# Sharing each gate/up chunk between the two row groups of TensorE, one chunk apart, in a spectral-mixing block with a GeGLU feed-forward

## The chip, the cores and the metric

One core of a Trainium2 chip; the sessions of experiments ran on three different chips. The metric is the device time of one execution in microseconds (us); lower is better. Executions of one kernel vary here by some 0.5%, so medians of several runs are given, and ratios are taken within one session on one chip; where times of different sessions are put side by side, the text says so. A trace is one execution under the profiler; its "span" runs from the first to the last instruction and lies 1.8 to 3.5 us (mostly 2.2) below the device time of the same execution. The engines are PE (TensorE, matmuls), DVE (VectorE), ACT (ScalarE), POOL (GpSimd) and SP (SyncE); SBUF is the memory on the core, PSUM the memory into which PE writes its sums, in banks. "Warm" means on the full granted clock of PE, "cold" on half of it.

## The reference, cut to what matters

```python
S, D, F = 2048, 576, 4608
x  = A_x                                              # bf16 [1, 2048, 576]
X  = rfft2(layernorm(x)) * (w_r + 1j * w_i)           # spectral mixing
h  = x + irfft2(X, s=(S, D))
n  = layernorm(h)
h2 = h + (gelu(n @ w_gate) * (n @ w_up)) @ w_down     # GeGLU feed-forward
```

The feed-forward (FFN) takes more than four fifths of the time. The size D = 576 over which gate and up sum is 4.5 times 128, or nine tiles of 64 features.

## The kernel before: the parts that matter

The spectral stage is built from matmuls with tables. Each of 16 groups passes D (columns), B (a 16-point transform and the weight multiply on DVE) and V (a 16-point inverse); V lags D by two groups:

```python
ZS = sb.alloc("ZS", [128, 2, 2, ZW], BF16)            # double buffer between B and V
for i in range(NG + 2):
    if i < NG:        st_D(i)
    if 1 <= i <= NG:  st_B(i - 1)                     # writes ZS[i % 2] on DVE
    if i >= 2:        st_V(i - 2)                     # PE reads ZS
```

Then 16 row tiles of 128 tokens pass the inverse stages `st_I` and `st_N` and the second layernorm. For the first block of 512 tokens, PE turns the normalised tile (`turn_pe`), DVE copies it out of PSUM, and two copies SBUF to SBUF double the activations, so that each of the nine 64-feature tiles lies on partitions 0-63 and again on partitions 64-127:

```python
HT0 = sb.alloc("HT0", [128, 9, 512], BF16)
def turn_pe(c):
    ...                                               # five 128x128 turns on PE into PSUM
    DVE: HT0[:, 0:5, t0:t1] <- PSUM                   # written short
    P.dma(SP, HT0[0:64, 5:9, t0:t1],   HT0[64:128, 0:4, t0:t1], ...)   # the doubling copies
    P.dma(SP, HT0[64:128, 5:9, t0:t1], HT0[0:64, 1:5, t0:t1], ...)
```

Blocks 2 to 4 are turned by nine DMA transposes a tile, while the block before them computes. The weights of gate lie on partitions 0-63, those of up on 64-127. Both are loaded early, from two queues, in nine pieces of 512 columns; the down weights follow on the POOL queue as soon as the spectral stage has freed their space:

```python
for j in range(9):
    f0, f1 = 512 * j, 512 * j + 512
    P.dma(POOL, WGU[0:64, :, f0:f1],   wgv[:, :, f0:f1], ...)
    P.dma(SP,   WGU[64:128, :, f0:f1], wuv[:, :, f0:f1], ...)
for j in range(9):
    P.dma(POOL, WD[:, 4 * j:4 * j + 4, :], wdv[...], ...)
```

A chunk is 128 of the 4608 inner features for 512 tokens. Gate runs on rows 0-63 of the array and up on rows 64-127, as nine pairs of matmuls that run at the same time into two PSUM banks:

```python
def gu(n, tb, f):
    b0 = 2 * (n % 3)
    for kt in range(9):
        for o in range(2):                            # 0: gate, 1: up
            h0, sl = 64 * o, (GT, UT)[o][kt]
            matmul(bank(b0 + o), WGU[h0:h0+64, kt, 128*f:128*f+128], HT[h0:h0+64, sl, :],
                   start=(kt == 0), stop=(kt == 8))
    if n == 0: st_N(15)                               # the last 128-point inverse
    ACT: GL <- gelu(bank(b0));   DVE: AT[:, f, :] <- GL * bank(b0 + 1)
```

36 chunks make a block; then `down` multiplies AT with the down weights (288 matmuls of 288 columns) and the output is stored. There are four blocks.

Of the kernel before, what the change touches and what calls it, by code (L numbers as in the profile page):

```python
# [4 lines left out]
BF16 = mybir.dt.bfloat16  # L5
# [137 lines left out]
class Prog:  # L143
# [12 lines left out]
    def op(self, eng, fn, r=(), w=(), dma=None):  # L156
# [6 lines left out]
        for k in w:  # L163
            for o in self.last_w.get(k, ()):
                deps.add((o, "waw"))
            for o in self.readers.get(k, ()):
                deps.add((o, "war"))
        op = _Op(eng, fn, deps, dma)
# [27 lines left out]
    def emit(self):  # L196
# [8 lines left out]
        for op in self.all:  # L205
            kn = known[op.eng]
            cand = {}
            for o, kind in op.deps:
                if o.dma is not None:
                    key, v = ("d", o.dma), o.val  # L210
                else:
                    if o.eng == op.eng and op.dma is None:
                        if op.eng == "pe":
                            continue
                    key, v = ("e", o.eng), o.pos + 1
                if v > kn.get(key, 0):
                    if key not in cand or v > cand[key][0]:
                        cand[key] = (v, o)
# [64 lines left out]
def _build(nc, A_x, A_w_r, A_w_i, B_w_gate, B_w_up, B_w_down, out):  # L283
# [39 lines left out]
    HT0 = sb.alloc("HT0", [128, 9, 512], BF16)  # L323
# [15 lines left out]
    ZS = sb.alloc("ZS", [128, 2, 2, ZW], BF16)  # L339
# [3 lines left out]
    HT1 = sb.alloc("HT1", [128, 9, 512], BF16)  # L343
# [189 lines left out]
    def st_B(i):  # L533
# [14 lines left out]
        P.op(DVE, lambda v, sl=sl: v.tensor_tensor(ZS[:, sl, 0, 0:KW], T1[:, sl, 0, :], T1[:, sl, 1, :], op=ALU.subtract), r=[("T1", sl)], w=[("Z", sl, 0)])  # L548
        P.op(DVE, lambda v, sl=sl: v.tensor_tensor(ZS[:, sl, 1, 0:KW], T2[:, sl, 0, :], T2[:, sl, 1, :], op=ALU.add), r=[("T2", sl, 0), ("T2", sl, 1)], w=[("Z", sl, 1)])  # L549

    def st_V(i):
        g = GORD[i]
        sl = i % 2
# [18 lines left out]
    for i in range(NG + 2):  # L572
# [4 lines left out]
        if i >= 2:  # L577
            st_V(i - 2)


    wgv = B_w_gate[:, :].rearrange("(t p) f -> p t f", p=64)
    wuv = B_w_up[:, :].rearrange("(t p) f -> p t f", p=64)
    wdv = B_w_down[:, :].rearrange("(c p) d -> p c d", p=128)
    for j in range(9):
        f0, f1 = 512 * j, 512 * j + 512
        P.dma(POOL, WGU[0:64, :, f0:f1], wgv[:, :, f0:f1], f"wg{j}", w=[("WG", j, 0)])
        P.dma(SP, WGU[64:128, :, f0:f1], wuv[:, :, f0:f1], f"wu{j}", w=[("WG", j, 1)])
# [3 lines left out]
    P.alias(["FT", "BT", "VT"], [("HT", 0, i, k) for i in range(4) for k in range(3)])  # L591
# [43 lines left out]
    def norm(c):  # L635
        hs = c % 2
        q = c // 4
        for i, (o0, o1, x0, x1) in enumerate(((0, D, 0, D), (D, 640, 0, 64))):
# [4 lines left out]
    def turn_dma(c):  # L643
# [3 lines left out]
        for k in range(9):  # L647
            o = 128 * k if k < 5 else 64 + 128 * (k - 5)
            P.dma(SP, HT[:, k, 128 * (c % 4):128 * (c % 4) + 128], HN[:, hs, o:o + 128], f"tr{c}",
                  r=[("HN", hs, 0), ("HN", hs, 1)], w=[("HT", q % 2, c % 4, k)], transpose=True)  # L650

    def turn_pe(c):
# [8 lines left out]
        P.dma(SP, HT0[0:64, 5:9, t0:t1], HT0[64:128, 0:4, t0:t1], f"tr{c}", r=[("HT", 0, c, 0)], w=[("HT", 0, c, 1)])  # L661
        P.dma(SP, HT0[64:128, 5:9, t0:t1], HT0[0:64, 1:5, t0:t1], f"tr{c}", r=[("HT", 0, c, 0)], w=[("HT", 0, c, 2)])

# [17 lines left out]
    fdead += [("T1", a) for a in range(2)] + [(n_, a, b_) for n_ in ("T2", "Z") for a in range(2) for b_ in range(2)]  # L681
    fnew = ([("AT", f) for f in range(36)] + [("GL", 0), ("GL", 1)] + [("HT", 1, i, k) for i in range(4) for k in range(9)])

    GT = (0, 5, 1, 6, 2, 7, 3, 8, 4)
    UT = (4, 0, 5, 1, 6, 2, 7, 3, 8)

    def gu(n, tb, f):
        b0 = 2 * (n % 3)
        HT = HTS[tb % 2]
        rk = [("HT", tb % 2, i, k) for i in range(4) for k in range(9)] + [("WG", f // 4, i) for i in range(2)]  # L690
        for kt in range(9):
            for o in range(2):
                h0, sl = 64 * o, (GT, UT)[o][kt]
                P.op(PE, lambda t, o=o, h0=h0, kt=kt, sl=sl, f=f, b0=b0, HT=HT: t.matmul(  # L694
                    bank(b0 + o), WGU[h0:h0 + 64, kt, 128 * f:128 * f + 128], HT[h0:h0 + 64, sl, :], start=(kt == 0), stop=(kt == 8)),
                    r=rk, w=[("PS", b0 + o)])
        if n == 0:
            st_N(NT - 1)
            P.alias(fdead, fnew)
        s2 = n % 2  # L700
# [4 lines left out]
    def down(tb, p):  # L705
        b0 = 6 - 2 * (p % 2)
        c = 4 * tb + p
        for h in range(2):
            for f in range(36):
                P.op(PE, lambda t, b0=b0, h=h, f=f, p=p: t.matmul(bank(b0 + h, 0, 128, 0, 288), AT[:, f, 128 * p:128 * p + 128],  # L710
                                                                  WD[:, f, 288 * h:288 * h + 288], start=(f == 0), stop=(f == 35)),
                     r=[("AT", f), ("WD", f // 4)], w=[("PS", b0 + h)])
            P.op(DVE, lambda v, b0=b0, h=h, p=p, c=c: v.tensor_tensor(OS[:, p % 2, 288 * h:288 * h + 288], bank(b0 + h, 0, 128, 0, 288),  # L713
                                                                      XO[:, c, 288 * h:288 * h + 288], op=ALU.add),
                 r=[("PS", b0 + h), ("X", c)], w=[("OS", p % 2, h)])
            P.dma(SP, ov[:, c, 288 * h:288 * h + 288], OS[:, p % 2, 288 * h:288 * h + 288], f"so{p % 2}{h}", r=[("OS", p % 2, h)], w=[("OUT", p % 2, h)])

    for tb in range(4):
        for f in range(36):
            gu(36 * tb + f, tb, f)  # L720
# [46 lines left out]
```

## Time and profile before

Median 527.12 us of three runs (525.86 to 527.65). The traced execution took 529.1 us, with a span of 526.9 us.

| stretch of the trace | from-to, us | what bounds it |
|---|---|---|
| spectral stage (D, B, V) | 21.6-65.2 | PE, but for 1.0 us at its start and about 2 us of waits at its end |
| inverse stages and layernorm | 65.2-90.7 | PE |
| nothing on PE | 90.7-98.8 | the doubling copies |
| FFN block 1, gate/up | 98.8-172.5 | PE, at first on half the clock |
| down 1, then blocks 2 to 4 | 172.5-526.9 | PE |

From the page of the kernel before: the span, each engine's busy time, the granted TensorE clock and the GB/s moved in 40 slices of 13.2 us, the chain that ended last, and the two groups of gate/up matmuls (busy us, mean ns of one, idle time just before them and what ended it). HT_69 is HT0 in the code, HT_84 is HT1; in later traces both are called HT.

```profile
span 526.9 us, 10210 instructions
...
PE 507.8 (96%) x4425; PEld 302.5 (57%) x4427; DVE 184.1 (35%) x428; ACT 152.8 (29%) x285; POOL 29.1 (6%) x49
...
PEclk9999999699999999999999999999999999999999
...
GB/s 289 247 208 230 220 268 316 68 11 26 26 25 7 13 18 18 11 26 24 26 9 12 17 18 11 27 27 26 6 12 18 18 1 1 0 1 2 12 18 18
...
PE PS L694 51%; PE PS L710 27%; PE PS L525 4%; PE PS L601 3%; SPq L191 2%; DMA XO<-in_A_x_dram 2%; PE PS L539 1%; SPq L193 1%; PE PS L558 1%; ACT U L453 1%; DMA HT_69<-HT_69 1%; PE PS L610 1%; PE PS L562 1%; DVE XO L613 1%; DMA HT_84<-HN 0%
...
L694 PE MATMUL PS<-HT_69,WGU 64*128 64x512 bf16 x1296 | 143.3, 380 | 8.2 <-DMA HT_69<-HT_69 8.1
...
L694 PE MATMUL PS<-HT_84,WGU 64*128 64x512 bf16 x1296 | 140.2, 376 | 0.0
```

PE is busy 96% of the span, and gate/up (L694) and down (L710) carry 78% of the chain. The one idle time of note stands in the first gate/up group: 8.1 us, ended by a DMA from HT to itself, that is, by a doubling copy. In the same slice, the eighth, the clock digit falls to 6. PE's waits from 60 to 110 us (total, times, longest) say it again, and show the end of the spectral stage:

```profile
PE PS L694 <- DMA HT_69<-HT_69: 8.1, 1, 8.1
PE PS L558 <- ACT YS L542: 0.8, 1, 0.8
PE PS L558 <- DVE ZS L549: 0.6, 1, 0.6
PE PS L601 <- ACT V L565: 0.5, 1, 0.5
```

The timeline of PE (start, length, operation, count) shows the hole between the last inverse matmul of the loop and the first gate/up, and behind it 18 matmuls in 4.02 us where a warm chunk takes 1.94:

```profile
90.29 0.41 PE L610 MATMUL PS<-GS,IT 128*128 128x288 bf16 x2
98.81 4.02 PE L694 MATMUL PS<-HT_69,WGU 64*128 64x512 bf16 x18 [8.11 <-DMA HT_69<-HT_69]
```

Stretches of the FFN (length, then busy time and count of PE, weight loads, DVE, ACT and POOL; then granted clock, DMA share and GB/s): the first 6.2 us run at a clock of 0.54, the rest at 1.00.

```profile
98.80:105.00 6.20, 6.20 (x30) 2.08 (x32) 0.77 (x2) 0.74 (x2) 0.00 (x0) 0.54 0.01 3
105.00:172.00 67.00, 66.92 (x621) 29.74 (x618) 26.58 (x47) 24.88 (x40) 0.00 (x0) 1.00 0.09 19
208.00:278.00 70.00, 70.00 (x649) 31.18 (x646) 26.63 (x44) 20.90 (x35) 0.00 (x0) 1.00 0.09 19
```

And the DMA issues of the weights and copies (count, size of one, median us from issue to landing):

```profile
WGU<-in_B_w_up_dram SPq DMA_DIRECT2D x9, 576.0 KB, 31.7
WD<-in_B_w_down_dram POOLq DMA_DIRECT2D x9, 576.0 KB, 18.0
...
HT_69<-HT_69 SPq DMA_DIRECT2D x8, 64.0 KB, 7.4
```

A copy of 64 KB takes 7.4 us in the median, from 3.5 to 17.1. By the trace's record of landings the last up load lands at 96.83 and the last copy at 98.45 us.

### The profile page before, as it was taken

How to read it: one execution, taken by the hardware profiler on the slowest of the kernel's cores; microseconds unless marked ns; L12 is line 12 of the kernel's file. 1: busy time of each engine (PE TensorE's matmuls, PEld its weight loads, DVE VectorE, ACT ScalarE, POOL GpSimd, SP SyncE). 2: the span in 40 equal slices, each digit the busy share in tenths (PEclk: the TensorE clock that was granted, in tenths of full speed). 3: DMA queues.
4: the chain of work that ended last, by engine and by line, in shares of the span. 5: the costliest groups of instructions: out<-in, count | busy, mean ns of one | idle time of the engine just before them, and what ended most of it. 6: DMA issues, size and time to landing. Idle time of an engine off the chain costs nothing.

```text
span 526.9 us, 10210 instructions
## 1 busy us (share of the span) xinstructions
PE 507.8 (96%) x4425; PEld 302.5 (57%) x4427; DVE 184.1 (35%) x428; ACT 152.8 (29%) x285; POOL 29.1 (6%) x49
## 2 busy tenths in 40 slices
PE   7899898499999999999999999999999999999997
PEld 3667576144444777444447774456677744444776
DVE  5677658044433111343331114433311133333111
ACT  5756578042343000223330002333300023333000
POOL 8800130000000000000000000000000000000000
PEclk9999999699999999999999999999999999999999
DMA  8999999401110000011100000111000000000000
GB/s 289 247 208 230 220 268 316 68 11 26 26 25 7 13 18 18 11 26 24 26 9 12 17 18 11 27 27 26 6 12 18 18 1 1 0 1 2 12 18 18
DMA packets 36812, 30.76 MB, mean 58 GB/s; under 512 B 21296, under 2 KB 32752, under 8 KB 36768
## 3 DMA queue, kind: packets, MB, share of 16 engines
q1 hardware_dynamic: 33312, 17.79, 14.8%
q0 software_dynamic: 3312, 11.80, 8.8%
q8 instruction: 35, 0.57, 0.5%
q10 hardware_dynamic: 144, 0.52, 0.3%
q14 instruction: 9, 0.07, 0.1%
HBM read 23.67 MB, written 2.36 MB: 49 GB/s over the span
## 4 chain that ended last, share of the span: by engine, by line
PE 88%; SPq 3%; DVE 3%; DMA 3%; ACT 2%; issue 1%; DVEq 0%; ACTq 0%
PE PS L694 51%; PE PS L710 27%; PE PS L525 4%; PE PS L601 3%; SPq L191 2%; DMA XO<-in_A_x_dram 2%; PE PS L539 1%; SPq L193 1%; PE PS L558 1%; ACT U L453 1%; DMA HT_69<-HT_69 1%; PE PS L610 1%; PE PS L562 1%; DVE XO L613 1%; DMA HT_84<-HN 0%
## 5 line engine op out<-in xcount | busy, mean ns | idle before, releaser
L701 ACT ACTIVATE GL<-PS 128x512 bf16<-128x512 f32 x144 | 85.8, 597 | 294.5 <-PE PS L694 293.0
L702 DVE TENSOR_TENSOR AT<-GL,PS 128x512 bf16<-128x512 bf16 x144 | 98.6, 687 | 167.1 <-ACT GL L701 167.1
L694 PE MATMUL PS<-HT_69,WGU 64*128 64x512 bf16 x1296 | 143.3, 380 | 8.2 <-DMA HT_69<-HT_69 8.1
L710 PE MATMUL PS<-WD,AT 128*128 128x288 bf16 x1152 | 141.8, 286 | 0.0
L694 PE MATMUL PS<-HT_84,WGU 64*128 64x512 bf16 x1296 | 140.2, 376 | 0.0
L710 PEld LDWEIGHTS PS<-WD,AT 128*128 128x128 bf16 x1152 | 112.4, 98 | 29.9 <-issue 1.7
L694 PEld LDWEIGHTS PS<-HT_69,WGU 64*128 64x128 bf16 x1296 | 70.8, 95 | 79.8 <-issue 11.7
L694 PEld LDWEIGHTS PS<-HT_84,WGU 64*128 64x128 bf16 x1296 | 62.6, 94 | 77.1 <-issue 0.5
L713 DVE TENSOR_TENSOR OS<-PS,XO 128x288 bf16<-128x288 f32 x32 | 14.6, 458 | 123.8 <-PE PS L710 123.8
L601 PE MATMUL PS<-DT,V 128*128 128x288 bf16 x160 | 22.0, 286 | 0.5 <-ACT V L565 0.5
L525 PE MATMUL PS<-FT,U 128*128 128x289 bf16 x160 | 22.3, 287 | 0.2 <-ACT U L453 0.2
L613 DVE SCALAR_TENSOR_TENSOR XO<-PS,XO 128x576 bf16<-128x576 f32 x16 | 12.1, 756 | 20.0 <-PE PS L610 19.8
L601 PEld LDWEIGHTS PS<-DT,V 128*128 128x128 bf16 x160 | 15.4, 98 | 4.3 <-issue 0.6
L525 PEld LDWEIGHTS PS<-FT,U 128*128 128x128 bf16 x160 | 14.4, 97 | 5.1 <-issue 0.4
L616 ACT ACTIVATE SQ<-XO 128x576 bf16<-128x576 bf16 x16 | 10.9, 682 | 15.3 <-DVE XO L613 15.1
L639 DVE TENSOR_SCALAR HN<-XO,TM,RS_59 128x576 bf16<-128x576 bf16 (+1 forms) x32 | 10.2, 360 | 8.8 <-DMA HT_84<-HN 6.4
L434 PE MATMUL PS<-ZD 128*128 128x512 bf16 x37 | 10.9, 447 | 1.5 <-POOL ZD L356 1.3
L558 PE MATMUL PS<-VT,ZS 128*128 128x256 bf16 x64 | 9.6, 271 | 2.4 <-DVE ZS L549 1.6
L405 DVE BATCH_NORM_STATS2 ST_53<-XO 128x6 f32<-128x288 bf16 x24 | 9.2, 443 | 5.5 <-DMA XO<-in_A_x_dram 5.5
L544 DVE TENSOR_TENSOR T_79<-YS,WS 128x580 bf16<-128x580 bf16 x16 | 7.4, 460 | 10.4 <-ACT YS L542 10.4
L603 ACT ACTIVATE GS<-PS 128x576 bf16<-128x576 f32 x16 | 10.2, 636 | 2.6 <-PE PS L601 2.6
L542 ACT ACTIVATE YS<-PS 128x578 bf16<-128x578 f32 x16 | 10.5, 655 | 1.5 <-PE PS L539 0.3
(57 smaller groups left out, 171.8 us busy)
## 6 DMA issues: line engine op xcount, KB each, us to landing
WGU<-in_B_w_gate_dram POOLq DMA_DIRECT2D x9, 576.0 KB, 25.8
WGU<-in_B_w_up_dram SPq DMA_DIRECT2D x9, 576.0 KB, 31.7
WD<-in_B_w_down_dram POOLq DMA_DIRECT2D x9, 576.0 KB, 18.0
out_dram<-OS SPq DMA_DIRECT2D x32, 72.0 KB, 1.6
XO<-in_A_x_dram SPq DMA_DIRECT2D x3, 576.0 KB, 8.0
HT_84<-HN SPq DMA_TRANSPOSE x72, 2.4
FT<-c_ftab SPq DMA_DIRECT2D x1, 725.0 KB, 12.5
DT<-c_dtab SPq DMA_DIRECT2D x1, 720.0 KB, 24.4
```

The source lines that it names most:

```text
L191: fn = lambda e: e.dma_start(out_ap, in_ap, transpose=True)
L434: P.op(PE, lambda t: t.matmul(bank(7), ZD[:, 0:128], ZD[:, :], start=True, stop=True), r=["ZD"], w=[("PS", 7)])
L525: P.op(PE, lambda t, b=b, o=o, dt=dt, g=g: t.matmul(bank(b, 0, 128, 0, K2), U[:, dt, g, :, :], FT[:, dt, o, 0:K2], start=(dt == 0), stop=( ...
L558: P.op(PE, lambda t, c=c, zp=zp, sl=sl, sp_=sp_: t.matmul(bank(6, 0, 128, 256 * c, 256 * c + 256), ZS[:, sl, zp, 128 * c:128 * c + 128], V ...
L601: P.op(PE, lambda t, b=b, h=h, kt=kt, c=c: t.matmul(bank(b, 0, 128, 0, 288), V[:, kt, c, :, :], DT[:, kt, 288 * h:288 * h + 288], start=(k ...
L613: P.op(DVE, lambda v, x2=x2, c=c: v.scalar_tensor_tensor(x2, banks(4, 2, 288), 1.0, x2, op0=ALU.mult, op1=ALU.add, accum_out=SB2[:, 0, c:c ...
L616: P.op(ACT, lambda a, sl=sl, c=c: a.activation(SQ[:, sl, :], XO[:, c, :], ACTF.Square, accum_out=SB2[:, 1, c:c + 1]), r=[("X", c)], w=[("S ...
L694: P.op(PE, lambda t, o=o, h0=h0, kt=kt, sl=sl, f=f, b0=b0, HT=HT: t.matmul(bank(b0 + o), WGU[h0:h0 + 64, kt, 128 * f:128 * f + 128], HT[h0 ...
L701: P.op(ACT, lambda a, s2=s2, b0=b0: a.activation(GL[:, s2, :], bank(b0), ACTF.Gelu_apprx_tanh), r=[("PS", b0)], w=[("GL", s2)])
L702: P.op(DVE, lambda v, s2=s2, b0=b0, f=f: v.tensor_tensor(AT[:, f, :], GL[:, s2, :], bank(b0 + 1), op=ALU.mult), r=[("GL", s2), ("PS", b0 + ...
L710: P.op(PE, lambda t, b0=b0, h=h, f=f, p=p: t.matmul(bank(b0 + h, 0, 128, 0, 288), AT[:, f, 128 * p:128 * p + 128], WD[:, f, 288 * h:288 * ...
L713: P.op(DVE, lambda v, b0=b0, h=h, p=p, c=c: v.tensor_tensor(OS[:, p % 2, 288 * h:288 * h + 288], bank(b0 + h, 0, 128, 0, 288), XO[:, c, 28 ...
```

## The change

Its intent: let each 64-feature tile be used where it lies, so that only the last one is needed twice. Even tiles stand on partitions 0-63, odd ones on 64-127, for gate and up alike; the ninth stands on both (the layernorm writes it twice), and rows 0-63 use it for gate, rows 64-127 for up. Rows 0-63 do the even half of a chunk's gate and up sums, rows 64-127 the odd half, into the same PSUM banks. So that both are never in one bank at once, rows 64-127 work one chunk behind, and PE waits on its own earlier matmul before the second half enters a bank. The doubling copies go, five transposes a tile take the place of nine, and the weights are loaded in four pieces over all 128 partitions. Apart from that, V lags three groups, and down's second pair of banks is 2 and 3 instead of 4 and 5. The diff is cut, and long calls are shortened.

```diff
-    HT0 = sb.alloc("HT0", [128, 9, 512], BF16)
+    HT0 = sb.alloc("HT0", [128, 5, 512], BF16)
-    ZS = sb.alloc("ZS", [128, 2, 2, ZW], BF16)
+    ZS = sb.alloc("ZS", [128, 3, 2, ZW], BF16)
...
-    for i in range(NG + 2):
+    for i in range(NG + 3):
...
-        if i >= 2:
-            st_V(i - 2)
+        if i >= 3:
+            st_V(i - 3)
...
-    for j in range(9):
-        f0, f1 = 512 * j, 512 * j + 512
-        P.dma(POOL, WGU[0:64, :, f0:f1], wgv[:, :, f0:f1], ...)
-        P.dma(SP, WGU[64:128, :, f0:f1], wuv[:, :, f0:f1], ...)
+    for j in range(4):
+        f0, f1 = 1152 * j, 1152 * j + 1152
+        for o, (eng, src) in enumerate(((POOL, B_w_gate), (SP, B_w_up))):
+            P.dma(eng, WGU[:, 4*o:4*o+4, f0:f1], src[0:512, f0:f1].rearrange("(t p) f -> p t f", p=128), ...)
+            P.dma(eng, WGU[64*o:64*o+64, 8, f0:f1], src[512:576, f0:f1], ...)
...
-        for k in range(9):                            # turn_dma
+        for k in range(5):
...
-        P.dma(SP, HT0[0:64, 5:9, t0:t1], HT0[64:128, 0:4, t0:t1], ...)
-        P.dma(SP, HT0[64:128, 5:9, t0:t1], HT0[0:64, 1:5, t0:t1], ...)
...
+    ASEQ = [(0, i) for i in range(4)] + [(0, 8)] + [(1, 4 + i) for i in range(4)]    # (gate/up, weight slot)
+    BSEQ = [(0, i) for i in range(4)] + [(1, 4 + i) for i in range(4)] + [(1, 8)]
+    def gu(n):
+        for j in range(9):
+            for half, m in ((0, n), (1, n - 1)):      # rows 64-127 are one chunk behind
+                if not 0 <= m < 144:
+                    continue
+                o, wt = (ASEQ, BSEQ)[half][j]
+                b = 2 * (m % 3) + o
+                aft = [half_done[m, o]] if half and (j == 0 or j == 4) else []       # PE waits on PE
+                op = matmul(bank(b), WGU[h0:h0+64, wt, ...], HT[h0:h0+64, kt, :],
+                            start=(half == 0 and j in (0, 5)), stop=(half == 1 and j in (3, 8)), after=aft)
+                if half == 0:
+                    half_done[m, o] = op
+        m = n - 1
...                                                   # gelu and product of chunk m
+    gu(0)                                             # one call more: half empty at both ends
     for tb in range(4):
         for f in range(36):
-            gu(36 * tb + f, tb, f)
+            gu(36 * tb + f + 1)
```

More of the change, by code (lines that the diff above doesn't have):

```diff
@@ L154, in __init__, with op @@
         self.dma_sems = {}
-    def op(self, eng, fn, r=(), w=(), dma=None):
+    def op(self, eng, fn, r=(), w=(), dma=None, after=()):
         if eng == "pool" and fn is not None and dma is None:
@@ L167, in op @@
                 deps.add((o, "war"))
+        for o in after:
+            deps.add((o, "self"))
         op = _Op(eng, fn, deps, dma)
@@ L212, in emit @@
                     if o.eng == op.eng and op.dma is None:
-                        if op.eng == "pe":
+                        if op.eng == "pe" and kind != "self":
                             continue
@@ L342, in _build @@
     AT = sb.alloc("AT", [128, 36, 512], BF16)
-    HT1 = sb.alloc("HT1", [128, 9, 512], BF16)
+    HT1 = sb.alloc("HT1", [128, 5, 512], BF16)
     GL = sb.alloc("GL", [128, 2, 512], BF16)
@@ L547, in st_B @@
                  r=[("Y", sl)] + wk, w=[("T2", sl, pl)])
-        P.op(DVE, lambda v, sl=sl: v.tensor_tensor(ZS[:, sl, 0, 0:KW], T1[:, sl, 0, :], T1[:, sl, 1, :], op=ALU.subtract), r=[("T1", sl)], w=[("Z", sl, 0)])
-        P.op(DVE, lambda v, sl=sl: v.tensor_tensor(ZS[:, sl, 1, 0:KW], T2[:, sl, 0, :], T2[:, sl, 1, :], op=ALU.add), r=[("T2", sl, 0), ("T2", sl, 1)], w=[("Z", sl, 1)])
+        P.op(DVE, lambda v, sl=sl: v.tensor_tensor(ZS[:, i % 3, 0, 0:KW], T1[:, sl, 0, :], T1[:, sl, 1, :], op=ALU.subtract), r=[("T1", sl)], w=[("Z", i % 3, 0)])
+        P.op(DVE, lambda v, sl=sl: v.tensor_tensor(ZS[:, i % 3, 1, 0:KW], T2[:, sl, 0, :], T2[:, sl, 1, :], op=ALU.add), r=[("T2", sl, 0), ("T2", sl, 1)], w=[("Z", i % 3, 1)])
     def st_V(i):
         g = GORD[i]
-        sl = i % 2
+        sl = i % 3
         sp_ = 1 if g == 0 else 0
@@ L576, in _build @@
             st_B(i - 1)
-        if i >= 2:
-            st_V(i - 2)
-    wgv = B_w_gate[:, :].rearrange("(t p) f -> p t f", p=64)
-    wuv = B_w_up[:, :].rearrange("(t p) f -> p t f", p=64)
+        if i >= 3:
+            st_V(i - 3)
     wdv = B_w_down[:, :].rearrange("(c p) d -> p c d", p=128)
-    for j in range(9):
-        f0, f1 = 512 * j, 512 * j + 512
-        P.dma(POOL, WGU[0:64, :, f0:f1], wgv[:, :, f0:f1], f"wg{j}", w=[("WG", j, 0)])
-        P.dma(SP, WGU[64:128, :, f0:f1], wuv[:, :, f0:f1], f"wu{j}", w=[("WG", j, 1)])
+    for j in range(4):
+        f0, f1 = 1152 * j, 1152 * j + 1152
+        for o, (eng, src) in enumerate(((POOL, B_w_gate), (SP, B_w_up))):
+            P.dma(eng, WGU[:, 4 * o:4 * o + 4, f0:f1], src[0:512, f0:f1].rearrange("(t p) f -> p t f", p=128), f"wgu{o}{j}", w=[("WG", j, o)])
+            P.dma(eng, WGU[64 * o:64 * o + 64, 8, f0:f1], src[512:576, f0:f1], f"wgu{o}{j}", w=[("WG", j, 2 + o)])
     P.alias(ukeys + wkeys[0] + wkeys[1] + ["Wz", ("CU", 0), ("CU", 1), ("SU", 0), ("SU", 1)], [("WD", j) for j in range(9)])
@@ L590, in _build @@
         P.dma(POOL, WD[:, 4 * j:4 * j + 4, :], wdv[:, 4 * j:4 * j + 4, :], f"wd{j}", w=[("WD", j)])
-    P.alias(["FT", "BT", "VT"], [("HT", 0, i, k) for i in range(4) for k in range(3)])
+    P.alias(["FT", "BT", "VT"], [("HT", 0, i, k) for i in range(4) for k in range(5)])
     vkeys = [("V", g) for g in range(NG)] + [("Vt", g) for g in range(NG)]
@@ L637, in norm @@
         q = c // 4
-        for i, (o0, o1, x0, x1) in enumerate(((0, D, 0, D), (D, 640, 0, 64))):
+        for i, (o0, o1, x0, x1) in enumerate(((0, D, 0, D), (D, 640, 512, D))):
             P.op(DVE, lambda v, c=c, hs=hs, o0=o0, o1=o1, x0=x0, x1=x1: v.tensor_scalar(HN[:, hs, o0:o1], XO[:, c, x0:x1], TM[:, 1, c:c + 1],
@@ L646, in turn_dma @@
         HT = HTS[q % 2]
-        for k in range(9):
-            o = 128 * k if k < 5 else 64 + 128 * (k - 5)
-            P.dma(SP, HT[:, k, 128 * (c % 4):128 * (c % 4) + 128], HN[:, hs, o:o + 128], f"tr{c}",
+        for k in range(5):
+            P.dma(SP, HT[:, k, 128 * (c % 4):128 * (c % 4) + 128], HN[:, hs, 128 * k:128 * k + 128], f"tr{c}",
                   r=[("HN", hs, 0), ("HN", hs, 1)], w=[("HT", q % 2, c % 4, k)], transpose=True)
@@ L660, in turn_pe @@
              r=[("PS", 6), ("PS", 7)], w=[("HT", 0, c, 0)])
-        P.dma(SP, HT0[0:64, 5:9, t0:t1], HT0[64:128, 0:4, t0:t1], f"tr{c}", r=[("HT", 0, c, 0)], w=[("HT", 0, c, 1)])
-        P.dma(SP, HT0[64:128, 5:9, t0:t1], HT0[0:64, 1:5, t0:t1], f"tr{c}", r=[("HT", 0, c, 0)], w=[("HT", 0, c, 2)])
     for c in range(NT + 1):
@@ L680, in _build @@
     fdead = vkeys + ["DT", "IT", ("G", 0), ("G", 1), ("Y", 0), ("Y", 1), "Yz", "Zz", ("SQ", 0), ("SQ", 1)]
-    fdead += [("T1", a) for a in range(2)] + [(n_, a, b_) for n_ in ("T2", "Z") for a in range(2) for b_ in range(2)]
-    fnew = ([("AT", f) for f in range(36)] + [("GL", 0), ("GL", 1)] + [("HT", 1, i, k) for i in range(4) for k in range(9)])
-    GT = (0, 5, 1, 6, 2, 7, 3, 8, 4)
-    UT = (4, 0, 5, 1, 6, 2, 7, 3, 8)
-    def gu(n, tb, f):
-        b0 = 2 * (n % 3)
-        HT = HTS[tb % 2]
-        rk = [("HT", tb % 2, i, k) for i in range(4) for k in range(9)] + [("WG", f // 4, i) for i in range(2)]
-        for kt in range(9):
-            for o in range(2):
-                h0, sl = 64 * o, (GT, UT)[o][kt]
-                P.op(PE, lambda t, o=o, h0=h0, kt=kt, sl=sl, f=f, b0=b0, HT=HT: t.matmul(
-                    bank(b0 + o), WGU[h0:h0 + 64, kt, 128 * f:128 * f + 128], HT[h0:h0 + 64, sl, :], start=(kt == 0), stop=(kt == 8)),
-                    r=rk, w=[("PS", b0 + o)])
-        if n == 0:
+    fdead += [("T1", a) for a in range(2)] + [(n_, a, b_) for n_ in ("T2", "Z") for a in range(3) for b_ in range(2)]
@@ new lines, in _build @@
+    fnew = ([("AT", f) for f in range(36)] + [("GL", 0), ("GL", 1)] + [("HT", 1, i, k) for i in range(4) for k in range(5)])
+    ASEQ = [(0, i) for i in range(4)] + [(0, 8)] + [(1, 4 + i) for i in range(4)]
+    BSEQ = [(0, i) for i in range(4)] + [(1, 4 + i) for i in range(4)] + [(1, 8)]
+    half_done = {}
+    def gu(n):
[3 more added lines that the diff above has]
+                    continue
+                tb, f = m // 36, m % 36
+                o, wt = (ASEQ, BSEQ)[half][j]
+                kt = 4 if wt == 8 else wt % 4
+                h0 = 64 * half
+                HT = HTS[tb % 2]
+                b = 2 * (m % 3) + o
+                aft = [half_done[m, o]] if half and (j == 0 or j == 4) else []
+                op = P.op(PE, lambda t, h0=h0, kt=kt, wt=wt, f=f, b=b, HT=HT, s=(half == 0 and j in (0, 5)), e=(half == 1 and j in (3, 8)): t.matmul(
+                    bank(b), WGU[h0:h0 + 64, wt, 128 * f:128 * f + 128], HT[h0:h0 + 64, kt, :], start=s, stop=e),
+                    r=[("HT", tb % 2, i, k) for i in range(4) for k in range(5)] + [("WG", f // 9, i) for i in range(4)],
+                    w=[("PS", b)], after=aft)
+                if half == 0:
+                    half_done[m, o] = op
+        m = n - 1
+        if m < 0:
@@ L698, in gu @@
             st_N(NT - 1)
             P.alias(fdead, fnew)
-        s2 = n % 2
+            return
+        s2, b0, f = m % 2, 2 * (m % 3), m % 36
         P.op(ACT, lambda a, s2=s2, b0=b0: a.activation(GL[:, s2, :], bank(b0), ACTF.Gelu_apprx_tanh), r=[("PS", b0)], w=[("GL", s2)])
@@ L705, in down @@
     def down(tb, p):
-        b0 = 6 - 2 * (p % 2)
         c = 4 * tb + p
         for h in range(2):
+            b = (6, 7, 2, 3)[2 * (p % 2) + h]
             for f in range(36):
-                P.op(PE, lambda t, b0=b0, h=h, f=f, p=p: t.matmul(bank(b0 + h, 0, 128, 0, 288), AT[:, f, 128 * p:128 * p + 128],
-                                                                  WD[:, f, 288 * h:288 * h + 288], start=(f == 0), stop=(f == 35)),
-                     r=[("AT", f), ("WD", f // 4)], w=[("PS", b0 + h)])
-            P.op(DVE, lambda v, b0=b0, h=h, p=p, c=c: v.tensor_tensor(OS[:, p % 2, 288 * h:288 * h + 288], bank(b0 + h, 0, 128, 0, 288),
-                                                                      XO[:, c, 288 * h:288 * h + 288], op=ALU.add),
-                 r=[("PS", b0 + h), ("X", c)], w=[("OS", p % 2, h)])
+                P.op(PE, lambda t, b=b, h=h, f=f, p=p: t.matmul(bank(b, 0, 128, 0, 288), AT[:, f, 128 * p:128 * p + 128],
+                                                                WD[:, f, 288 * h:288 * h + 288], start=(f == 0), stop=(f == 35)),
+                     r=[("AT", f), ("WD", f // 4)], w=[("PS", b)])
+            P.op(DVE, lambda v, b=b, h=h, p=p, c=c: v.tensor_tensor(OS[:, p % 2, 288 * h:288 * h + 288], bank(b, 0, 128, 0, 288),
+                                                                    XO[:, c, 288 * h:288 * h + 288], op=ALU.add),
+                 r=[("PS", b), ("X", c)], w=[("OS", p % 2, h)])
             P.dma(SP, ov[:, c, 288 * h:288 * h + 288], OS[:, p % 2, 288 * h:288 * h + 288], f"so{p % 2}{h}", r=[("OS", p % 2, h)], w=[("OUT", p % 2, h)])
+    gu(0)
     for tb in range(4):
         for f in range(36):
-            gu(36 * tb + f, tb, f)
+            gu(36 * tb + f + 1)
             if tb == 0 and f == 20:
```

## The prediction

> **What bounds the kernel now.** TensorE. The page gives PE 96% busy; the chain of waits puts 51% of 526.9 us on gate/up matmuls and 27% on down. Gate (rows 0-63) and up (rows 64-127) already run as pairs: in the timeline a pair starts every 215.5 ns when warm, so a chunk of nine pairs takes 1.945 us and a block of 36 takes 70.04 us (blocks 2 to 4 agree within 0.07 us). The Trainium skill, "TensorE: Matmul & The Clock Gate" (Back-to-back issue gap), gives 216 ns for 512 columns; the trace agrees. The change keeps nine slots per chunk, so the steady rate cannot improve. Down (122.5 ns each, 35.4 us per block) is untouched. What can be won lies outside the steady state:
>
> 1. Before the first gate/up matmul PE idles 8.1 us (waits view: on the DMA HT<-HT). DVE had the activations at 89.45 us, but the eight doubling copies queue behind the last up-weight loads, which land at 96.83; the last copy lands at 98.45.
> 2. That idle time halves the granted clock until about 104.5 us (PEclk row). The first block takes 73.67 us to its first down matmul instead of 70.04. The inserted last 128-point inverse explains 0.53; some 3.1 us are cold clock (pairs at 425 ns) and one 0.24 us stall at 139 us, where DVE's norm waited for a tile's nine transposes (1.25 us each).
> 3. In the spectral stage PE waits 1.0 us for the first ZS (26.5 to 27.46), then 0.8, 0.6 and 0.5 us at the drain (62 to 65.2). Between, a step takes 2.51 us and is PE-bound.
>
> **What the change does.**
> - No doubling copies: the first chunk needs DVE's HT and the first weight piece. That piece is larger (1152 columns), but from the first loads' landings I estimate it to land near 60 us. The loop's last matmul starts at 90.41, so the chunk can start at 90.6: -8.2 us.
> - No idle time, so no cold clock; five transposes instead of nine (6.3 us against 7.8 us between norms) remove the DVE stall: -3.1 us.
> - Lag 3 fills the first wait; the drain is 0.2 us worse through the single V bank: -0.8 us.
> - Skew: 145 calls of nine slots instead of 144: +1.94 us.
> - Two PE-on-PE waits per chunk, needed because row groups must not meet in a bank (the skill, "TensorEngine Tiling (Array Packing)", Gotcha 1). The awaited matmul lies four pairs back (0.86 us); a matmul takes 0.38 us and ACT starts about 0.1 us after PE, so I estimate 0.5 us to spare: 0.
> - Evacuation of a chunk has one chunk-time instead of two, but 0.60 + 0.69 us fit: 0. After each down, bank 3 is needed soon: +0.1 in all.
>
> Sum: -10.1 us, nearly all on the critical path. **Predicted 516.9 us, 80% range 514.8 to 520.3.** That is 1.9% faster, so the 2% line is near a coin toss: faster by over 2% 0.42, within 2% 0.54, slower 0.04.
>
> **Right if:** no PE wait before the first gate/up matmul, at about 89.8 us; clock 1.0 there; the wait on HT<-HT gone; chunk step still 1.945 us; blocks 2 to 4 unchanged; one extra 1.9 us at the first half chunk.
>
> **Wrong if:** the PE-on-PE waits drain the matmul queue (50 ns a chunk would cost 7 us); the first weights or late spectral weights land late with the new load shapes; single-row-group matmuls run slower; ACT's table switch at chunk 20 stalls PE.

## The result, and the profile after

The changed kernel takes 518.12 us (median of four runs, 517.97 to 518.41), the kernel before 527.38 us (four runs, 525.86 to 527.74). The ratio is 0.983, with a 95% interval of 0.981 to 0.985: faster by 1.7%, inside the 2% line. All ratios here are the mean time of one kernel's fast runs over that of the other's of the same rounds, so they are not quite the ratio of the quoted medians. All experiments below are recorded as correct.

The same lines of the page:

```profile
span 516.4 us, 10131 instructions
...
PE 507.4 (98%) x4425; PEld 295.9 (57%) x4427; DVE 184.5 (36%) x428; ACT 152.7 (30%) x285; POOL 27.8 (5%) x48
...
PEclk9999999999999999999999999999999999999999
...
GB/s 289 289 343 307 208 361 44 4 24 22 7 1 2 18 18 11 22 22 11 1 1 18 18 11 20 22 15 1 1 13 18 18 1 1 0 2 1 13 18 17
...
PE PS L699 55%; PE PS L720 27%; PE PS L527 4%; PE PS L602 3%; DMA XO<-in_A_x_dram 2%; PE PS L541 1%; ACT U L455 1%; PE PS L560 1%; PE PS L611 1%; PE PS L564 1%; DVE XO L614 0%; ACT JNK L400 0%; DVE ST_53 L407 0%; ACT JNK L402 0%; ACT YS L544 0%
...
L699 PE MATMUL PS<-HT_69,WGU 64*128 64x512 bf16 x1296 | 144.4, 376 | 0.0
L699 PE MATMUL PS<-HT_84,WGU 64*128 64x512 bf16 x1296 | 144.4, 376 | 0.0
```

No gate/up group has idle time before it, the clock is never below 9 tenths, and gate/up and down are 82% of the chain. In the sixth slice the DMA moves 361 GB/s, and from the eighth on the weight traffic is over. PE's waits from 60 to 110 us; the wait for HT is gone:

```profile
PE PS L564 <- DVE V L569: 1.0, 2, 0.5
PE PS L602 <- ACT V L567: 0.5, 1, 0.5
```

The timeline. The first nine matmuls, on one row group, start at 89.56, 0.2 us after the last matmul of the loop before; then comes the moved-in inverse, and then the steady stream:

```profile
89.22 0.41 PE L611 MATMUL PS<-GS,IT 128*128 128x288 bf16 x2
89.56 2.11 PE L699 MATMUL PS<-HT_69,WGU 64*128 64x512 bf16 x9
91.61 0.42 PE L611 MATMUL PS<-GS,IT 128*128 128x288 bf16 x2
91.96 0.82 PE L699 MATMUL PS<-HT_69,WGU 64*128 64x512 bf16 x6
```

The windows (columns as above): no cold stretch.

```profile
89.60:92.00 2.40, 2.40 (x14) 0.89 (x15) 0.77 (x2) 1.57 (x5) 0.00 (x0) 1.00 0.00 0
92.00:162.00 70.00, 70.00 (x650) 31.42 (x649) 27.45 (x49) 26.20 (x42) 0.00 (x0) 1.00 0.05 11
```

The weight loads reach their places sooner: in the median an up piece, now twice as large, lands 22.5 us after its issue instead of 31.7, a down piece after 9.3 instead of 18.0:

```profile
WD<-in_B_w_down_dram POOLq DMA_DIRECT2D x9, 576.0 KB, 9.3
...
WGU<-in_B_w_up_dram SPq DMA_DIRECT2D x4, 1152.0 KB, 22.5
```

Where the 10.5 us between the two traces went, from the start times of the matmuls:

| stretch | before | after | difference | predicted |
|---|---|---|---|---|
| start to first D | 21.61 | 21.80 | +0.2 | 0 |
| first D to first inverse matmul | 43.63 | 42.36 | -1.3 | -0.8 |
| first to last inverse matmul of the loop | 25.18 | 25.18 | 0.0 | 0 |
| last inverse matmul of the loop to first gate/up | 8.39 | 0.22 | -8.2 | -8.2 |
| first gate/up to first down | 73.67 | 72.43 | -1.2 | -3.1 + 1.9 |
| first down to end | 354.4 | 354.4 | 0.0 | +0.1 |
| span | 526.9 | 516.4 | -10.5 | -10.1 |

### The profile page after: what moved, and what is told of

It is laid out like the page before. It is cut to its first block, busy times and chain, and to the rows that moved or that the text cites. A ratio compares the mean times of both kernels' runs of the same rounds, so it can differ in the third digit from the quotient of the medians.

```text
span 516.4 us, 10131 instructions
## 1 busy us (share of the span) xinstructions
PE 507.4 (98%) x4425; PEld 295.9 (57%) x4427; DVE 184.5 (36%) x428; ACT 152.7 (30%) x285; POOL 27.8 (5%) x48
## 4 chain that ended last, share of the span: by engine, by line
PE 93%; DVE 2%; ACT 2%; DMA 2%; issue 0%; SPq 0%; DVEq 0%
PE PS L699 55%; PE PS L720 27%; PE PS L527 4%; PE PS L602 3%; DMA XO<-in_A_x_dram 2%; PE PS L541 1%; ACT U L455 1%; PE PS L560 1%; PE PS L611 1%; PE PS L564 1%; DVE XO L614 0%; ACT JNK L400 0%; DVE ST_53 L407 0%; ACT JNK L402 0%; ACT YS L544 0%
## 5 line engine op out<-in xcount | busy, mean ns | idle before, releaser
L699 PE MATMUL PS<-HT_69,WGU 64*128 64x512 bf16 x1296 | 144.4, 376 | 0.0
L699 PE MATMUL PS<-HT_84,WGU 64*128 64x512 bf16 x1296 | 144.4, 376 | 0.0
L699 PEld LDWEIGHTS PS<-HT_84,WGU 64*128 64x128 bf16 x1296 | 64.5, 94 | 77.9 <-issue 0.5
L699 PEld LDWEIGHTS PS<-HT_69,WGU 64*128 64x128 bf16 x1296 | 64.5, 94 | 76.8 <-issue 0.7
L544 ACT ACTIVATE YS<-PS 128x578 bf16<-128x578 f32 x16 | 10.5, 655 | 1.8 <-PE PS L541 0.7
L541 PE MATMUL PS<-CUS,BT 128*128 128x289 bf16 x64 | 10.6, 286 | 0.2
L533 ACT ACTIVATE CUS<-PS 128x289 bf16<-128x289 f32 x16 | 6.6, 413 | 14.0 <-PE PS L527 14.0
## 6 DMA issues: line engine op xcount, KB each, us to landing
WGU<-in_B_w_up_dram SPq DMA_DIRECT2D x4, 1152.0 KB, 22.5
```

The source lines that it names most:

```text
L541: P.op(PE, lambda t, b=b, o=o, tb=tabs[o], sl=sl, sp_=sp_: t.matmul(bank(b, 0, 128, 0, K2), BT[:, sp_, tb, :], CUS[:, sl, o, 0:K2], start= ...
L544: P.op(ACT, lambda a, sl=sl: a.activation(YS[:, sl, :, 0:K2], banks(4, 2, K2), ACTF.Copy), r=[("PS", 4), ("PS", 5)], w=[("Y", sl)])
L699: op = P.op(PE, lambda t, h0=h0, kt=kt, wt=wt, f=f, b=b, HT=HT, s=(half == 0 and j in (0, 5)), e=(half == 1 and j in (3, 8)): t.matmul(ban ...
```

## The experiments

The trace fits the prediction nearly line by line. Open is why. The prediction held that the copies were late because they stood in line behind the up loads, and that longer rows make the loads faster. If that is all, the row-group scheme is not needed: a better order of loads would do. The theory and its rivals were tested on parts of the change.

### The kernel before once more (b2)

No edit.

> The kernel before, unchanged, for a second trace of it. The first trace came from an execution of 529.1 us, while its unprofiled runs have a median of 527.4, so about 1.7 us of what I read in it may be particular to that execution. My theory: the idle time before the first gate/up matmul and the cold-clock time after it vary from run to run (they depend on when the queued copies land[...]); everything else agrees within 0.2 us. I expect idle 6 to 9 us and a first block 71 to 74 us. Rival: idle and cold clock are the same again (8.1 and 73.7) and the surplus is elsewhere.

Measured: 526.03 us, one run (state unknown, as for every single run here). PE's wait:

```profile
PE PS L694 <- DMA HT<-HT: 4.2, 1, 4.2
```

The wait was 4.2 us, not 8.1. In this trace the last up load landed at 94.94 instead of 96.83, and the loop before ended at 92.9 instead of 90.7: 0.5 us of that had come before the spectral stage, and 1.7 since the clock had been at half for 3.41 us from 65.8 on, within the inverse stage. The wait is thus 3.9 us shorter, but the first gate/up matmul starts only 1.7 us earlier (97.07 against 98.81). The first block took 72.38 us. So the idle time (below the 6 to 9 expected) and the cold part vary from run to run, and with them the kernel's time; the fast runs of before in all sessions lie between 525.4 and 528.6 us. The first trace's execution, 529.1 us, lies just above that range.

### Only the lag of three (e1_lag3)

```diff
-    ZS = sb.alloc("ZS", [128, 2, 2, ZW], BF16)
+    ZS = sb.alloc("ZS", [128, 3, 2, ZW], BF16)
-    for i in range(NG + 2):
+    for i in range(NG + 3):
-        if i >= 2:
-            st_V(i - 2)
+        if i >= 3:
+            st_V(i - 3)
```

> The kernel before with nothing but the three-deep ZS and the inverse lagging three groups. Theory: the first 1.0 us wait is filled, the spectral stage ends 0.8 to 1.1 us earlier; but the first gate/up matmul still waits for the doubling copies, which wait for the up weights and not for the spectral stage, so the kernel gains nothing: within 0.5 us of before. Rival (gains add up): 0.9 us faster.

Measured: 528.43 us against 526.55 of before, ratio 1.003 (0.999 to 1.007): the same.

```profile
PE PS L694 <- DMA HT<-HT: 9.9, 1, 9.9
PE PS L562 <- DVE V L567: 1.0, 2, 0.5
```

The waits at the drain are those of the changed kernel, so the lag did its work, and the loop ended at 89.7 us, 1.0 earlier than in the first trace of before. But the first gate/up matmul started at 99.61, and the wait grew to 9.9 us. Work saved ahead of a wait that something else sets is given back in that wait. Theory held: in the changed kernel the 1.3 us of the lag can count only because the copies are gone (the changed kernel with a lag of two was not run).

### Wide weight rows in the kernel before (e3_wide), narrow ones in the changed kernel (e4_after_narrow)

```diff
 # e3_wide, on the kernel before (dependencies follow)
-    for j in range(9):
-        f0, f1 = 512 * j, 512 * j + 512
+    for j in range(4):
+        f0, f1 = 1152 * j, 1152 * j + 1152
 # e4_after_narrow, on the changed kernel: the reverse
```

> The kernel before with nothing changed but the shape of the gate and up loads: four pieces of 1152 columns (rows of 2304 bytes) instead of nine of 512 (rows of 1024 bytes). Doubled activations, copies, pairing of gate and up all stay. Theory: the copies were late only because they stood behind the up loads; these now land near 62 us as in the changed kernel, the copies land 2 to 3 us after DVE's tile at 89.5, the idle time falls from 8 to 1 to 2 us and the clock stays full: 517 to 519 us, nearly the whole gain of the change without its row-group scheme. Rival: the copies themselves are slow (7.4 us from issue to landing): idle at least 5 us, 523 us or more.

> The changed kernel with the weight loads cut back to nine pieces of 512 columns (1024-byte rows), everything else as changed. Theory: without copies nothing waits for the last up load, and the first piece lands early; the up loads end near 95 us again, but the time stays within 0.5 us of the changed kernel (518.1). Rival: the gain of the change came from the faster weight loads, and this one falls back by 2 us or more.

Measured: e3_wide 526.13 us against 526.55 (ratio 0.998, 0.994 to 1.001): nothing gained. **My theory was wrong**, in both halves. The up loads moved hardly more bytes a second (below), and the copies took longer still:

```profile
WGU<-in_B_w_up_dram SPq DMA_DIRECT2D x4, 1296.0 KB, 43.2
...
HT<-HT SPq DMA_DIRECT2D x8, 64.0 KB, 11.0
```

The last up load landed at 89.99 instead of about 96, but the last copy landed only at 98.12, and the first gate/up matmul started at 98.48. e4_after_narrow took 518.19 us (ratio to before 0.984, 0.981 to 0.987), the changed kernel's time: its 1024-byte rows cost nothing, and its weights landed by 81.5 us, as with 2304-byte rows (81.0).

So the row length does not set the rate. The last numbers in the following windows are GB/s, each in a stretch in which the up loads run all but alone. The kernel before (1024-byte rows on 64 partitions):

```profile
60.00:66.00 6.00, 4.02 (x37) 2.37 (x36) 3.65 (x15) 3.19 (x6) 2.39 (x4) 1.00 1.13 200
```

e3_wide (2304-byte rows, 64 partitions):

```profile
60.00:66.00 6.00, 4.03 (x33) 2.11 (x31) 3.71 (x15) 3.24 (x6) 2.33 (x4) 0.84 1.05 205
```

The changed kernel (2304-byte rows, 128 partitions):

```profile
50.00:60.00 10.00, 9.93 (x89) 7.03 (x86) 7.60 (x29) 6.21 (x12) 0.00 (x0) 1.00 1.03 290
```

e4_after_narrow (1024-byte rows, 128 partitions):

```profile
50.00:60.00 10.00, 9.93 (x89) 7.02 (x87) 7.61 (x29) 6.37 (x13) 0.00 (x0) 1.00 1.12 302
```

It is the partitions: 200 and 205 GB/s on 64 of them, 290 and 302 on 128. The Trainium skill says so: "SBUF — State Buffer", section "Door 1: The DMA port swizzle", has partitions 0-63 reach 8 of 16 ports and gives 196 GB/s for them at 1 MiB against 328 for all 128. These traces agree with the first figure and come to nine tenths of the second. I had not looked there before predicting. Two sections further that page ("Can I just issue two DMAs to hit both halves?") says that two transfers to the two halves at once hardly help (6%). The kernel before loads gate into one half and up into the other at once, and moved 211 GB/s from 28 to 48 us (table loads included), while the changed kernel moved 327.

### The copies in another queue (e2_actq)

```diff
-        P.dma(SP, HT0[0:64, 5:9, t0:t1], ...)
-        P.dma(SP, HT0[64:128, 5:9, t0:t1], ...)
+        P.dma(ACT, HT0[0:64, 5:9, t0:t1], ...)
+        P.dma(ACT, HT0[64:128, 5:9, t0:t1], ...)
```

> The kernel before with only the eight doubling copies issued from the scalar engine's queue instead of the sync engine's, while the narrow up loads go on as before. Theory: the copies were late because they stood in line behind the up loads of their own queue; from another queue they land within 4 us of issue although the DMA engines are as busy as before, and the idle time falls below 4 us (the issues cost the scalar engine some time in the inverse stage, so the stage may stretch by 1 to 4 us). Rival: the engines are saturated, and the copies still take 7 us or more.

Measured: 526.96 us, one run. The copies took no less time in a queue in which nothing stands before them:

```profile
HT<-HT ACTq DMA_DIRECT2D x8, 64.0 KB, 9.6
```

The rival held: 9.6 us from issue to landing. The wait for them shrank to 2.6 us only because the stage before had grown; PE waited there for the slowed ACT:

```profile
PE PS L610 <- ACT GS L603: 3.3, 3, 1.3
PE PS L694 <- DMA HT<-HT: 2.6, 1, 2.6
```

This agrees with "DMA: Bandwidth & Descriptors", section "Rules for kernel authors", of the skill: spreading DMAs over issuing engines gives no bandwidth, since all use the same 16 DMA engines. Put beside each other, the traces that have the copies beside weight traffic show one pattern. The copies end 1.2 to 1.8 us after the weight traffic of all queues:

| run | last weight load lands | last copy lands | first gate/up starts |
|---|---|---|---|
| before | 96.83 (up) | 98.45 | 98.81 |
| b2 | 94.94 (up) | 96.72 | 97.07 |
| e1_lag3 | 97.59 (up) | 99.26 | 99.61 |
| e2_actq | 96.15 (up) | 97.34 | 97.69 |
| e3_wide | 96.76 (down) | 98.12 | 98.48 |
| e8_filler (below) | 96.69 (up) | 98.35 | 98.73 |
| e9_wide_lag3 | 93.72 (down) | 95.02 | 95.38 |

### Wide rows and the lag (e9_wide_lag3)

Both edits above, on the kernel before.

> The kernel before with the wide weight rows and the lag of three, still with doubled activations and gate/up on fixed row groups. Theory: with the copies no longer late the lag's 0.9 us now counts; left against the changed kernel are 1 to 2 us of waiting for the last copies, and the missing skew pays 1.9 back: 516.5 to 518.5 us, the same as the changed kernel within 1 us. Rival: the row-group scheme itself is worth something, and this stays 2 us or more behind the changed kernel.

Measured: 525.53 us against 526.4, ratio 0.998 (0.995 to 1.000); the rival came true, 7.4 us behind the changed kernel's 518.12, which is of another session (the ratios to before are 0.998 and 0.983). The up loads had ended by 82.99 us, yet the copies waited for the end of the down loads (table). With that, standing behind the up loads is ruled out as the cause.

### The down loads kept away from the copies (e10_wd_late)

```diff
-    for j in range(9):
-        P.dma(POOL, WD[...], wdv[...], f"wd{j}", w=[("WD", j)])
...                                                   # after the loop of inverse stages:
+    for j in range(9):
+        P.dma(POOL, WD[...], wdv[...], f"wd{j}", r=[("HT", 0, c, k) for c in range(4) for k in (1, 2)], w=[("WD", j)])
```

> The kernel before with one thing moved: the nine down-weight loads (5.3 MB, not needed before about 160 us) wait until the doubling copies have landed, instead of running beside the up loads and the copies. Copies, their queue, the narrow up loads and the order of everything else stay. New theory, after the wide rows and the other queue did not help: the copies land late in whichever queue because the DMA engines are full; in seven traces the first gate/up matmul starts 1.5 to 2.1 us after the last of all weight loads. With the down loads away the up loads end near 82 us, the last copies land 2 to 3 us after the last tile's DVE copy, the idle time falls to 1.5 to 2.5 us, and the cold part of the first block mostly goes: 519.5 to 522 us. Rival: the copies are slow by themselves or behind the up loads, and it stays above 524.5 us.

Measured: 520.95 us against 527.4, ratio 0.988 (0.985 to 0.990), as expected of the new theory.

```profile
WGU<-in_B_w_up_dram SPq DMA_DIRECT2D x9, 576.0 KB, 16.6
...
HT<-HT SPq DMA_DIRECT2D x8, 64.0 KB, 2.1
```

The same copies in the same queue behind the same narrow up loads land in 2.1 us; the up loads, from 60 us on alone on the DMA engines, were through at 80.44 us. PE's wait shrinks with them:

```profile
PE PS L695 <- DMA HT<-HT: 1.9, 1, 1.9
```

Together with e2_actq and e9_wide_lag3 this shows what the copies waited for: the weight traffic, whichever queue carries it, and not their place in line. The DMA engines were full while they waited (busy share 1.04 from 72 to 88 us in before, 0.52 from 70 to 92 here); how the engines share their time out, so that a copy issued at 79.76 in e2_actq landed only at 95.09, is not shown. It also shows how far a reordering gets without the row-group scheme: some 70% of the gain (6.5 of 9.3 us). The last copy of 2.1 us stays on the critical path, and this version was not joined with the lag. Its trace also has half the clock for 3.41 us from 64.84 on, as b2 has. Such a stretch at the end of the spectral stage is in five of the eight traces of before and its variants, and in none of the six of the changed kernel and its variants. It may be part of what is left between the two (2.8 us, of different sessions); no run separates it.

### Slow weight loads in the changed kernel (e11_half_loads)

```diff
-    for j in range(4):
+    for h in range(2):
+      for j in range(4):
...
-            P.dma(eng, WGU[:, 4*o:4*o+4, f0:f1], src[0:512, f0:f1]..., ...)
+            p0 = 64 * (h ^ o)
+            P.dma(eng, WGU[p0:p0+64, 4*o:4*o+4, f0:f1], (same rows of p0:p0+64), ...)
```

> The changed kernel with each gate and up load cut into one for partitions 0-63 and one for 64-127 (gate does the low half first, up the high half first); same bytes, same 2304-byte rows, same places. Theory: what slowed the weight traffic before was that each load wrote 64 partitions only (alone it ran at 200 GB/s with 1024-byte and with 2304-byte rows; with 128 partitions at 300 with both): the up loads now run at about 200 GB/s when alone and all weights land at 93 to 98 us instead of 81, and yet the time stays within 0.5 us of the changed kernel (518.1 us), since no copy waits for them. Rival A: the rate has another cause and stays near 300. Rival B: slower traffic costs time even without copies, 2 us or more.

Measured: 518.98 us (517.61 to 519.34), ratio to before 0.984 (0.982 to 0.986), where e4_after_narrow had 0.984 and the change itself 0.983. The median is 0.9 us above the changed kernel's of another session, a little outside the 0.5 I allowed; the four spans, 515.6 to 516.9 us, lie around the changed kernel's 516.0 to 516.4. With 64 partitions a load, the up loads fall to the old rate:

```profile
60.00:66.00 6.00, 4.50 (x42) 2.88 (x40) 2.82 (x12) 2.96 (x5) 4.12 (x6) 1.00 1.04 212
```

All weights are in by 96.4 us, as late as before the change, and PE does not wait. So the faster loads that came with the change are not what pays; that nothing small must pass through them is.

### Dummy matmuls against the cold clock (e8_filler)

```diff
+    for _ in range(28):
+        matmul(bank(7), IDT, XO[:, 0, 0:512], start=True, stop=True)   # result unused
     for tb in range(4):
```

> The kernel before with 28 dummy matmuls of 512 columns (about 6.0 us) put before the first gate/up matmul, in the time in which PE waits for the copies anyway. Theory: the clock stays full, so the first block loses its cold part: 2.5 to 3 us faster than before, 524.5 us, with the wait for the copies unchanged. Rival: the slow first block is not the clock but waits inside it, and the time stays at 527.

Measured: 526.93 us against 526.4, ratio 1.000 (0.997 to 1.002). The trace shows the intended effect, 18 matmuls in 2.12 us instead of 4.02:

```profile
91.83 6.21 PE L719 MATMUL PS<-XO,IDT 128*128 128x512 bf16 x28
98.73 2.12 PE L694 MATMUL PS<-HT,WGU 64*128 64x512 bf16 x18 [0.70 <-DMA HT<-HT]
```

The first block took 70.98 us, against 73.67 and 72.38 in the two traces of before; so the cold clock is worth 1.4 to 2.7 us there. But the start lay at 98.73 us in this trace, with the up loads landing at 96.69, and no gain is seen in the median. The landing varies by as much as the effect. As a measure of time this experiment is inconclusive; its trace shows only that the first block is fast when the clock is full.

### A shorter lag between the row groups (sk7, sk5)

```diff
-            for half, m in ((0, n), (1, n - 1)):      # 9 slots behind
+        for half, q in ((0, n), (1, n - SKEW)):       # n counts slots; SKEW = 7 or 5
```

> The changed kernel with the second row group lagging by 7 slots instead of 9, so that each wait of PE on PE is for a matmul 3 slots (0.65 us) back instead of 5. Theory: a matmul's 0.38 us plus 0.1 to 0.2 us for the semaphore fit in 0.65 us, so no stall; two slots of skew less save 0.43 us. Rival: the waits already cost something at 9 slots, and shorter distance makes every chunk slower, by 20 ns or more (3 us in all).

> The changed kernel with a lag of 5 slots: each of the 288 waits of PE on PE is for the matmul one slot (0.216 us) back. Theory: from the start of the awaited matmul to the start of the one that waits pass 0.5 to 0.6 us, so each wait stalls 0.3 to 0.4 us and the kernel takes 90 to 115 us more. Rival: the waits are cheap or the queue hides them, and it takes less than 20 us more.

Measured: sk7 518.57 us, sk5 525.49 us, one run each. From the first gate/up matmul to the end sk7 took 426.42 us, the changed kernel 426.85: the two slots less are gained and nothing stalls. With a lag of 5 the weight loads wait for PE's own matmuls (total, times, longest):

```profile
PEld PS L701 <- PE PS L701: 97.0, 284, 0.3
```

These 97.0 us are mostly idle time of weight loads that overlap running matmuls. From first gate/up to end, sk5 took 433.8 us, 6.9 more than the changed kernel, though it has four slots (0.86 us) less to do: 7.8 us for 288 waits, 27 ns each. The start times show two slots around each wait lengthened by 8 to 14 ns. My estimate of 0.3 to 0.4 us of stall was far too high; the theory of 90 us falls, and the rival holds. For the changed kernel both say the same: five slots away, these waits cost nothing.

### Swapping within a pair of chunks instead of lagging (e5_pairs)

```diff
+    def first(m):                                     # 5 slots: rows 0-63 gate, rows 64-127 up
+    def second(m):                                    # 4 slots: rows 0-63 up, rows 64-127 gate
+    def pair(n):
+        for m in (n, n + 1): first(m)
+        if n == 0: st_N(15)
+        for m in (n, n + 1): second(m)                # then gelu and product of chunk m
...
-            b = (6, 7, 2, 3)[2 * (p % 2) + h]         # down's banks
+            b = 2 * p + h
```

> The changed kernel with another order of the same half-tile matmuls: two chunks make a unit; in its first ten slots rows 0-63 do gate and rows 64-127 do up of one chunk, then of the other; in the last eight slots they swap. Each bank is still touched by one row group at a time, with four pairs between the last write of one group and the first of the other, but no chunk lags, so no half-empty calls at either end. Theory: the skew costs one call of nine slots (1.94 us) and nothing else, so this takes 516.2 us (518.1 - 1.9), 0.979 of before. Rival: the order costs elsewhere (two evacuations at once, waits that come in bursts), and it is no faster than the changed kernel.

Measured: 517.42 us (516.62 to 519.22), ratio to before 0.983 (0.980 to 0.985). In the trace the half-empty call is gone; the first ten slots run in pairs, the inverse follows, and then the swap:

```profile
89.35 2.33 PE L691 MATMUL PS<-HT,WGU 64*128 64x512 bf16 x20
91.61 0.42 PE L611 MATMUL PS<-GS,IT 128*128 128x288 bf16 x2
91.97 2.33 PE L691 MATMUL PS<-HT,WGU 64*128 64x512 bf16 x20
```

From the start of the first gate/up matmul to that of the last down matmul it takes 421.93 us, against 423.87 in the changed kernel: 1.94 us less, which is what one call of nine slots costs. The spans are 514.3 to 515.7 us against 516.0 to 516.4 of the changed kernel. The device times differ by 0.7 us in the medians, of different sessions, which their scatter does not resolve. So it is the fastest of the kernels here by its trace, and by its time not provably faster than the changed one.

## Why the prediction was right or wrong, point by point

- *TensorE bounds it, and the steady rate cannot improve.* Right. A chunk takes 1.94 us before and after; blocks 2 to 4 did not move.
- *No wait before the first gate/up matmul, start at 89.8 us.* Right: 89.56.
- *Clock full, first block 3.1 us shorter, skew 1.94 us dearer.* Right: the block fell by 1.24 us, the balance of both. Nine slots on one row group took 1.95 us (217 ns each).
- *Lag 3: -0.8 us.* Right in kind, too small: -1.3. The drain did get a new wait, on DVE's evacuation of the last columns (twice 0.5 us), but it replaced older ones of 0.8 and 0.6, so that the drain became 0.4 us better and not 0.2 worse. e1_lag3 shows that this gain exists only once the copies are gone.
- *PE-on-PE waits: 0.* Right in size. The reason given, 0.5 us to spare out of 0.86, rested on some 0.4 us from an awaited matmul to the next; sk5, which waits for the matmul one slot (0.216 us) back, loses 27 ns a wait and so shows far less.
- *516.9 us; measured 518.12.* In the range, 1.2 us low: a gain of 10.1 us was forecast and 9.3 measured. The term of the sum that was mis-sized is the idle time with its cold clock, -8.2 and -3.1 us: read from one trace of an execution of 529.1 us and taken from a median of 527.1. A second trace had 4.2 us of wait and a first block of 72.38. Between the traces the change is worth 10.5 us, between the medians 9.3.
- *"The eight doubling copies queue behind the last up-weight loads."* Wrong as a cause, though nothing in the sum hung on it. e2_actq gave them another queue and they took 9.6 us; e9_wide_lag3 ended the up loads at 83 and they still landed at 95; e10_wd_late took the down loads away and they landed in 2.1 us. The DMA engines were full, and the copies ended with the traffic. Part of it was true, without setting the end: in the first trace DVE's last tile was ready at 89.45 and SP issued its two copies only at 93.39 and 94.94, while in e9_wide_lag3 (90.34, then 90.37 and 91.00) nothing held them, and they still landed 1.3 us after the last load.
- *"The first weight piece" in time.* Right, and earlier than the estimated 60 us: both parts of up's first piece had landed at 49.4 us. What makes the loads faster is the number of partitions (e3_wide, e4_after_narrow, e11_half_loads).

Open remain three things. How long the clock stays low after a wait was not separated cleanly in time (e8_filler). Whether e10_wd_late with the lag would catch up with the changed kernel was not run. And that two row groups in one bank at once go wrong, the reason for the lag, rests on the skill ("TensorEngine Tiling (Array Packing)", Gotcha 1) alone: no run here shows it, since taking the waits away would be a race.

## What to carry to other kernels

When PE waits for a small copy, look at what all queues move at that time before changing the copy's queue; a load that is not needed for 60 us can hold up the one that is needed now, and the cure is to issue it later, or to need no copy. A gain ahead of such a wait is worth nothing until the wait is gone. And take the baseline for a prediction from the same executions as the waits that are subtracted from it: one trace shows one draw of them.

## What the Trainium skill lacked or had wrong

- "DMA: Bandwidth & Descriptors" gives no time for a small SBUF-to-SBUF copy through these engines beside full-rate weight loads. Here the median 64 KB copy took 2.1 us with the engines free and 7.3 to 11.0 us beside weight loads, in either queue.
- "SBUF — State Buffer" has the 64-partition rate right (196 GB/s there, 200 to 212 here, with 1024-byte and with 2304-byte rows), and that two halves at once hardly help (211 GB/s here). For 128 partitions these traces show 290 to 302 GB/s alone, below its 328.
- "TensorE: Matmul & The Clock Gate", Back-to-back issue gap, gives about 131 ns a matmul as the sustained rate of load-and-multiply streams with 512 columns. Here such a stream ran at 217 ns on one row group, and at 215.5 ns a pair on two; its formula for the single gap (216 ns) is what fits.
- The same page's table of advice ties the fall of the clock to idle gaps longer than about 3 us; another of its sections says that short idle times between groups of matmuls can do it too, but gives no share of busy time. In b2 the clock was at half for 3.41 us from 65.8 us on, and the longest idle gap of PE in the ten microseconds before was 0.8 us; it was busy for 1.67 of the 3.40 us from 62.3.
- No page says what a wait of PE on its own earlier matmul costs. Here: nothing at a distance of three or five slots, 27 ns at one.
